# Linear attention and SwiGLU, two layers: the column sums of phi(K) from a matmul of ones, or from the gram product itself

## The chip, the cores and the metric

The kernel runs on one core of a Trainium2 chip. The core has a matrix engine (PE, TensorE), three engines for elementwise work (DVE is VectorE, ACT is ScalarE, POOL is GpSimd), a queue processor that issues the transfers (SP) and 16 DMA engines. Every engine works through its own list of instructions in order and waits on semaphores for the others. Matmuls take their operands from on-chip memory (SBUF) and write to eight banks of accumulators (PSUM).

The metric is the device time of one execution in microseconds, as the median of several runs. All times below are microseconds unless marked ns.

## What is computed

`x` has 2048 rows of 512 features. Two kinds of block are applied in turn, A, B, A, B, and each adds its result to `x`.

```python
def _A_ref(x, wqkv, wo):                       # H = 32 heads of 16
    q, k, v = ...                              # x @ wqkv, split by head
    phi = lambda t: jnp.where(t > 0, t + 1, jnp.exp(t)) + 1e-6
    pq, pk = phi(q), phi(k)
    kv = jnp.einsum("bhsd,bhse->bhde", pk, v)
    z = jnp.einsum("bhsd->bhd", pk)            # column sums of phi(K)
    num = jnp.einsum("bhqd,bhde->bhqe", pq, kv)
    den = jnp.einsum("bhqd,bhd->bhq", pq, z)[..., None] + 1e-6
    return (num / den) @ wo                    # heads put side by side again

def _B_ref(x, w1, w3, w2):
    return (silu(x @ w1) * (x @ w3)) @ w2      # 512 -> 1792 -> 512

x = x + _A_ref(layernorm(x), A_wqkv, A_wo)
x = x + _B_ref(layernorm(x), B_w1, B_w3, B_w2)
# and both once more with the same weights
```

`z`, the 512 column sums of phi(K) over the 2048 rows, is the quantity that the change is about.

## The kernel before

The rows are worked on in 16 tiles of 128. Every fp32 operand of a matmul is split into a high and a low fp16 part, and a product is three passes, high by high, low by high and high by low (`PASSES`, line 32, and `mm`, line 873). All working buffers are views of one large tile, `arena`, so most names in the profile are `arena`.

A layer of attention (`attention`, line 1244) has three stages.

*Keys.* For tile t, `keys_rows` and `keys_turn` (lines 1483 and 1491) normalise the rows (ACT, line 855), cast them to the high part (`nat[:, 0]`, POOL or ACT, lines 790 and 792), form the low part (`nat[:, 1]`, DVE or POOL, line 1497) and transpose both by DMA (line 1498). The transposed tile times the key weights is `pk` (12 matmuls of 512 columns, line 878, into the tile named `pk`). `phi_act` and `phi_sum` (lines 1222 and 1236) make phi(K) of it in three ACT instructions (lines 1228 to 1230) and one DVE instruction (line 1239). ACT scales it to its high part (line 1306), DVE makes the low part (line 1321). `gram` (line 1269) multiplies the transpose of the untransposed normalised rows `nat` by phi(K), 512 by 512 numbers added up over all 16 tiles in the four banks `gt0` to `gt3`; that is 12 matmuls of 512 columns a tile. The values never appear: since V is the normalised rows times the value weight, kv is the value weight's transpose times this gram matrix.

*The state.* The column sums, wanted in every partition, stand in the bank `pz`. `gram_sum` (line 1257) adds a tile to them on PE, as a matmul with a matrix of ones, once with the high and once with the low part. A table, `pz:` in `ENGINES` (lines 543 and 551), says for each tile who adds it: E is PE, P and V are POOL and DVE, which add phi(K) in fp32 to `pksum` (lines 1310 and 1312). In layer 0 the first 12 tiles are E and the last 4 P; in layer 1 there are 14 P and 2 V and no E. `totals` (line 1345) brings what `pksum` holds into `pz` with one fp32 matmul, which the trace shows as two instructions. From `pz` come a power of two per column that scales the gram matrix (`inverse` and `scale_gram`, lines 752 and 1359), the row `zb` for the denominators (line 1366) and the columns that scale the output weights (lines 1368, 1374, 1382). The scaled gram matrix is split (lines 1360 and 1363) and multiplied by the value weight (`kv`, 48 small matmuls of line 878), masked to heads, split again and multiplied by the output weight (`pm`).

*Queries.* Four tiles ahead, `query` makes `pq`, DVE, ACT and POOL make phi(Q), weigh it and divide it, a DMA transposes it, and `po` is the product with `pm`. Between the end of the gram and the first product with the state, PE has the first query tiles to do.

The MLP follows with 7 groups of hidden features in chunks of 512 rows, with fewer products than the plain formula has. It takes most of the time and isn't touched.

During the keys of layer 0 the weights come in from HBM and are prepared. `att_piece` (line 1979) loads the attention weights, `prepare_vo` (line 1012) finds the largest value of the value and output weights (DVE, line 720), and splits them (ACT line 800, DVE line 802). The tables `FILLS` say how many such steps follow which step of the keys; each `yield` of `prepare_vo` is one step.

The order of the instructions on every engine is written out by hand: `ORDER` (line 72) holds, for each of PE, DVE, ACT, POOL and SP, the order as a permutation of the order in which the program records them, and `arrange` (line 634) pins it. On each engine, then, a late instruction holds up all that stand behind it.

Of the kernel before, what the change touches and what calls it, by code (L numbers as in the profile page):

```python
# [8 lines left out]
F16 = mybir.dt.float16  # L9
# [441 lines left out]
def kernel(  # L451
# [792 lines left out]
    def attention(layer, ready, prep, before_gram):  # L1244
# [36 lines left out]
        for t in range(NT):  # L1281
# [8 lines left out]
            if t == lag:  # L1290
                gt.extend([acc_bank(f"gt{j}") for j in range(NK)])
                if "E" in sums:
                    pz.append(bank("pz"))
# [799 lines left out]
```

## Time and profile before

| | before |
|---|---|
| median of 3 runs | 1154.07 (1153.33 to 1154.54) |
| the profiled execution, its own time | 1151.51 |
| its span, first to last instruction | 1149.8 |
| PE busy | 1139.5 (99%) |
| DVE busy | 822.0 (71%) |
| ACT busy | 628.8 (55%) |
| POOL busy | 405.8 (35%) |
| granted TensorE clock | 1.00 |

The profiled execution took 2.56 less than the median of the runs, and 1.7 of its own time lies outside the span. Layer 0's keys run from the start to about 105, its queries to about 195, its MLP to about 590; layer 1 follows with its keys to about 669, and its last instructions are the stores of the output.

Rows of the page and of the trace name a line of the kernel, an engine, an operation, the tile written and the tiles read (`arena<-arena`), the shape and type, and the count. Rows of the timeline begin with start and duration; what ended the idle time before an instruction stands in brackets. A busy time merges overlaps: consecutive matmuls overlap in the pipeline, so a matmul's own duration (379 ns at 512 columns) is longer than the distance from one to the next.

### The profile page before, as it was taken

How to read it: one execution, taken by the hardware profiler on the slowest of the kernel's cores; microseconds unless marked ns; L12 is line 12 of the kernel's file. 1: busy time of each engine (PE TensorE's matmuls, PEld its weight loads, DVE VectorE, ACT ScalarE, POOL GpSimd, SP SyncE). 2: the span in 40 equal slices, each digit the busy share in tenths (PEclk: the TensorE clock that was granted, in tenths of full speed). 3: DMA queues.
4: the chain of work that ended last, by engine and by line, in shares of the span. 5: the costliest groups of instructions: out<-in, count | busy, mean ns of one | idle time of the engine just before them, and what ended most of it. 6: DMA issues, size and time to landing. Idle time of an engine off the chain costs nothing.

```text
span 1149.8 us, 21802 instructions
## 1 busy us (share of the span) xinstructions
PE 1139.5 (99%) x8862; PEld 864.0 (75%) x8862; DVE 822.0 (71%) x1401; ACT 628.8 (55%) x1078; POOL 405.8 (35%) x472
## 2 busy tenths in 40 slices
PE   8999999999999999999999999999999999999998
PEld 3445445888888888888854454478888888888887
DVE  6888888977878986778774467847866676556533
ACT  6587878866544554334457644776554434343422
POOL 4533688411101312212568615771153110303111
PEclk9999999999999999999999999999999999999999
DMA  9975666875854221111314715674253440022001
GB/s 277 316 231 201 183 171 129 229 170 180 242 203 182 99 84 65 65 65 66 92 32 128 216 41 122 120 172 93 77 134 116 169 174 1 28 80 101 1 19 56
DMA packets 163397, 147.43 MB, mean 128 GB/s; under 512 B 129632, under 2 KB 138976, under 8 KB 158688
## 3 DMA queue, kind: packets, MB, share of 16 engines
q1 hardware_dynamic: 163296, 146.04, 44.3%
q8 instruction: 69, 1.13, 0.4%
q14 instruction: 32, 0.26, 0.1%
HBM read 72.48 MB, written 42.07 MB: 100 GB/s over the span
## 4 chain that ended last, share of the span: by engine, by line
PE 94%; POOL 3%; DMA 1%; DVE 1%; ACT 1%; issue 0%; SPq 0%; POOLq 0%
PE bb L878 25%; PE po L1739 18%; PE bc L878 13%; PE pq L878 7%; PE po L878 7%; PE ba L878 6%; PE gt L878 6%; PE pk L878 5%; PE po L1759 4%; DMA arena<-arena 1%; DMA arena<-in_A_x_dram 1%; POOL arena L1312 0%; PE kv L878 0%; PE pm L878 0%; PE pz L1261 0%; POOL rs_all L849 0%
## 5 line engine op out<-in xcount | busy, mean ns | idle before, releaser
L878 PEld LDWEIGHTS <-arena 128*128 128x128 f16 x6360 | 617.8, 98 | 242.5 <-DMA arena<-arena 6.6
L878 PE MATMUL bb<-arena 128*128 128x256 f16 x2688 | 348.7, 273 | 0.1
L1739 PE MATMUL po<-arena 128*128 128x256 f16 x1932 | 266.7, 273 | 0.0
L1692 ACT ACTIVATE arena<-bb 128x512 f32<-128x512 f32 x196 | 115.8, 593 | 226.0 <-PE bb L878 186.5
L1739 PEld LDWEIGHTS <-arena 128*128 128x128 f16 x1932 | 189.0, 98 | 22.3
L878 PE MATMUL bc<-arena 128*128 128x256 f16 x1344 | 178.9, 273 | 0.0
L1695 DVE TENSOR_TENSOR arena<-arena,bc 128x512 f32<-128x512 f32 x112 | 76.7, 685 | 102.5 <-PE bc L878 56.6
L1653 DVE TENSOR_TENSOR arena<-arena 128x512 f16<-128x512 f32 (+1 forms) x90 | 104.4, 1162 | 32.1 <-ACT arena L1651 32.1
L1647 ACT ACTIVATE arena<-arena,scalars 128x512 f32<-128x512 f32 (+1 forms) x112 | 74.5, 666 | 96.2 <-DVE arena L1695 87.0
L1651 ACT ACTIVATE arena<-arena 128x512 f16<-128x512 f32 (+1 forms) x112 | 98.9, 886 | 33.5 <-DVE arena L1666 13.1
L1788 DVE SCALAR_TENSOR_TENSOR arena<-po,scalars,arena 128x256 f32<-128x256 f32 (+1 forms) x170 | 94.6, 584 | 27.5 <-PE po L1739 18.9
L1648 DVE SCALAR_TENSOR_TENSOR arena<-arena,scalars 128x512 f32<-128x512 f32 (+1 forms) x112 | 80.9, 723 | 39.4 <-ACT arena L1647 38.0
L878 PE MATMUL ba<-arena 128*128 128x256 f16 x672 | 92.1, 273 | 0.0
L878 PE MATMUL pk<-arena 128*128 128x512 f16 x384 | 87.8, 379 | 3.3 <-DMA arena<-arena 3.3
L878 PE MATMUL gt<-arena 128*128 128x512 f16 x384 | 88.9, 379 | 0.8 <-ACT arena L1306 0.6
L878 PE MATMUL pq<-arena 128*128 128x512 f16 x384 | 86.6, 379 | 0.0
L878 PE MATMUL po<-arena 128*128 128x512 f16 x384 | 86.5, 379 | 0.0
L1808 POOL TENSOR_TENSOR arena<-arena 128x512 f32<-128x512 f32 x25 | 34.1, 1366 | 114.7 <-DVE arena L1788 114.7
L1653 POOL TENSOR_TENSOR arena<-arena 128x512 f16<-128x512 f32 x22 | 27.0, 1225 | 124.2 <-ACT arena L1651 84.5
L1809 POOL TENSOR_TENSOR arena<-arena 128x512 f32<-128x512 f32 x25 | 37.0, 1479 | 84.0 <-DVE arena L1788 83.9
L1759 PE MATMUL po<-arena 128*128 128x256 f16 x480 | 64.8, 273 | 0.0
L855 ACT ACTIVATE arena<-arena,nb_all,rs_all 128x512 f32<-128x512 f32 x64 | 51.0, 805 | 17.4 <-POOL nb_all L852 14.4
(163 smaller groups left out, 1286.1 us busy)
## 6 DMA issues: line engine op xcount, KB each, us to landing
arena<-xb_d SPq DMA_DIRECT2D x12, 1792.0 KB, 7.7
xb_d<-arena SPq DMA_DIRECT2D x8, 1792.0 KB, 7.5
xt_d<-arena SPq DMA_DIRECT2D x32, 256.0 KB, 3.3
arena<-xt_d SPq DMA_DIRECT2D x32, 256.0 KB, 3.1
arena<-in_B_w_dram SPq DMA_DIRECT2D x8, 896.0 KB, 6.6
arena<-in_B_w_dram SPq DMA_DIRECT2D x28, 256.0 KB, 3.1
w_d<-arena SPq DMA_DIRECT2D x4, 1792.0 KB, 9.5
arena<-w_d SPq DMA_DIRECT2D x4, 1792.0 KB, 7.4
```

The lines of the kernel that those rows point to most:

```text
L855: nc.scalar.activation(dst, x_sb[:, t, :], AF.Identity, scale=rs_all[:, t : t + 1], bias=nb_all[:, t : t + 1],)
L878: nc.tensor.matmul(dst, lhs(a, k), rhs(b, k), start=first and k == 0 and i == 0, stop=last and k == n - 1 and i == len(PASSES) - 1, skip_g ...
L1647: nc.scalar.activation(t, gate, AF.Silu, scale=info["u1"])
L1648: nc.vector.scalar_tensor_tensor(t, up, info["hid"], t, OP.mult, OP.mult)
L1651: nc.scalar.activation(hs[:, 0, lo:hi], t[:, lo:hi], AF.Copy)
L1653: engine.tensor_tensor(hs[:, 1, lo:hi], t[:, lo:hi], hs[:, 0, lo:hi], OP.subtract)
L1692: nc.scalar.activation(dst, bank_, AF.Copy)
L1695: nc.vector.tensor_tensor(dst, dst, bank_, OP.add)
L1739: nc.tensor.matmul(po[:, i * HALF : (i + 1) * HALF], hs[:, a, qx, cs], w2[:, b, qw, :], start=g == ends[0] and i + a + b == 0, stop=g == e ...
L1759: nc.tensor.matmul(acc[n][:, half * HALF : (half + 1) * HALF], hs[:, a, qx, cs], w2_a21[g][:, b] if (i, half) == (0, 1) else w2[:, b, i + ...
L1788: nc.vector.scalar_tensor_tensor(dst, src, cb, to, OP.mult, OP.add)
L1809: engine.tensor_tensor(x1, x1, u[:, 1:], OP.add)
```

## The change

The gram product delivers the column sums itself. Its row for feature 0 is the sum over the rows of `nat[:, feature 0]` times phi(K). If that column of `nat` is set to ones (1 in the high part, 0 in the low part) after the tile has been transposed, row 0 of the gram matrix is the column sums of phi(K). The true row of feature 0 is then missing. It isn't needed if the value weight's first row is zero, and it can be made so: a normalised row sums to zero over its features, so subtracting one row of the weight from all its rows leaves the product as it is.

- `gram_sum`, the table `pz:` and `pksum` go, with their 24 matmuls (layer 0), 2 copies and 16 additions on POOL and 2 additions on DVE.
- `gram` begins with a copy of two numbers into each of 128 partitions of `nat`, on POOL: 16 in each layer. The first group of a tile's matmuls (`gt0`) needs it, the other three don't.
- `totals` copies the bank `gt0` to SBUF on ACT, and the fp32 matmul multiplies it by a matrix that picks its first row. Before, this matmul read `pksum`. The bank `pz` is taken there and no longer at the first tile of layer 0.
- One more DMA brings the first row of the value weight to all 128 partitions, 256 KB written, and `prepare_vo` subtracts it from the four pieces of the weight on POOL before their largest value is taken. This adds four steps to `prepare_vo`.
- Two small memsets on DVE make the pair (1, 0).
- `ORDER` is written anew for all five engines, over the whole kernel.

```diff
-            "pz:EEEEEEEEEEEEPPPP plain:YYNN ...
+            "plain:YYNN ...
...
-            "pz:PPPPPPPPPPPVVPPP plain:NNNYNNNY ...
+            "plain:NNNYNNNY ...
...
+    first_one = scalar().bitcast(F16)
+    nc.vector.memset(first_one[:, 0:1], 1.0)
+    nc.vector.memset(first_one[:, 1:2], 0.0)
...
-    pksums = view(AT_T + 2 * KB, F32, D), junk_row
...
+    v_first = view(AT_W + 8 * KB, F32, D)
...
     def prepare_vo():
         yield AT["v"]
+        for k in range(NK):
+            nc.gpsimd.tensor_tensor(st_att[2][:, k, :], st_att[2][:, k, :], v_first, OP.subtract)
+            yield 1
         yield from attn_bound("v", 2)
...
-        def gram_sum(t):
-            if sums[t] == "E":
-                pk = pks[t]
-                for a in range(2):
-                    nc.tensor.matmul(
-                        pz[0],
-                        ones16,
-                        pk[:, a, :],
...
-                    )
-
         def gram(t):
             pk, nat = pks.pop(t), nats.pop(t)
+            nc.gpsimd.tensor_copy(nat[:, :, 0], first_one)
             for j in range(NK):
...
-                if "E" in sums:
-                    pz.append(bank("pz"))
...
             def high():
                 nc.scalar.activation(pk[:, 0, :], e, AF.Copy, scale=info["tk"])
-                if sums[t] != "E":
-                    engine = engine_of("pz", t)
-                    if t == rows_of[0]:
-                        engine.tensor_copy(pksum, e)
-                    else:
-                        engine.tensor_tensor(pksum, pksum, e, OP.add)
...
         def totals():
             held["rz"] = f32()
-            if not pz:
-                pz.append(bank("pz"))
-            if rows_of:
-                factor = info["tk"].to_broadcast([P, P])
-                nc.tensor.matmul(pz[0], factor, pksum, start=len(rows_of) == NT, stop=True)
+            pz.append(bank("pz"))
+            nc.scalar.activation(junk_row, gt[0], AF.Copy)
+            pick = one_row.to_broadcast([P, P])
+            nc.tensor.matmul(pz[0], pick, junk_row, start=True, stop=True)
...
     def att_piece(i):
         src = wqkv_r[:, i] if i < 3 else wo.rearrange("(k p) n -> p k n", p=P)
+        if i == 2:
+            nc.sync.dma_start(v_first, wqkv[0:1, 2 * D :].to_broadcast([P, D]))
```

Feature 0 of a row has left the gram product by this, and only there: the keys and the queries are made from the transposed tiles, which hold all features.

More of the change, by code (lines that the diff above doesn't have):

```diff
@@ L542 @@
         (
-            "pz:EEEEEEEEEEEEPPPP plain:YYNN hid:VPVVVVPVPPVVVVPVPPPPPPPVVPVV "
+            "plain:YYNN hid:VPVVVVPVPPVVVVPVPPPPPPPVVPVV "
             "den:AVAAVVVVVAAAAAAV bq:AAVV nat:APAPAPPPPPPAAAAA key:PPPPAPPPPPPPPPAA "
@@ L550 @@
         (
-            "pz:PPPPPPPPPPPVVPPP plain:NNNYNNNY hid:VVVVVVPPVPVVVVVVVVVVPVVPPPPP "
+            "plain:NNNYNNNY hid:VVVVVVPPVPVVVVVVVVVVPVVPPPPP "
             "den:VVVVVAVVAAVVVVVV nat:AAAPPPPAPAAAAAAA key:AAAAAPPPAAAAPAAP "
@@ L1250, in attention @@
         gt, pz, pks = [], [], {}
-        sums = table_of("pz", layer)
-        rows_of = [t for t in range(NT) if sums[t] != "E"]
-        pksum = pksums[layer]
-        def gram_sum(t):
-            if sums[t] == "E":
-                pk = pks[t]
-                for a in range(2):
-                    nc.tensor.matmul(
-                        pz[0],
-                        ones16,
-                        pk[:, a, :],
-                        start=t == sums.index("E") and a == 0,
-                        stop=not rows_of and t == NT - 1 and a == 1,
-                    )
         def gram(t):
             pk, nat = pks.pop(t), nats.pop(t)
+            nc.gpsimd.tensor_copy(nat[:, :, 0], first_one)
             for j in range(NK):
@@ L1296, in attention @@
             if lag < t < LATER:
-                gram_sum(t - 1)
                 gram(t - 1)
             elif t > LATER:
-                gram_sum(t - 2)
                 gram(t - 2)
@@ L1427, in attention @@
         chain = {
-            "gram14": lambda: (gram_sum(NT - 2), gram(NT - 2)),
-            "gram15": lambda: (gram_sum(NT - 1), gram(NT - 1)),
+            "gram14": lambda: gram(NT - 2),
+            "gram15": lambda: gram(NT - 1),
             "totals": totals,
```

701 rows, old and new, of the table ORDER are left out of this document.

## The prediction

> **What bounds the kernel now.** I read the page first, then who waited for whom on PE, then the windows of layer 0's keys, and last the timeline at the places that the change touches.
>
> ```profile
> span 1149.8 us, 21802 instructions
> PE 1139.5 (99%) x8862; PEld 864.0 (75%) x8862; DVE 822.0 (71%) x1401; ACT 628.8 (55%) x1078; POOL 405.8 (35%) x472
> ...
> PE 94%; POOL 3%; DMA 1%; DVE 1%; ACT 1%; issue 0%; SPq 0%; POOLq 0%
> ```
>
> PE is busy for 99% of the span and carries 94% of the chain that ended last. In such a kernel a matmul less is worth its distance to the next one, as long as PE finds its next work ready. The waits of PE and three windows (columns: window, its length, busy time and count of PE, PEld, DVE, ACT and POOL, clock, DMA share, GB/s) say how ready it is:
>
> ```profile
> PE pk L878 <- DMA arena<-arena: 3.3, 4, 1.4
> PE gt L878 <- ACT arena L1306: 0.6, 1, 0.6
> PE gt L878 <- DVE arena L1321: 0.2, 1, 0.2
> ...
> 24.00:104.47 80.47, 80.10 (x375) 36.98 (x374) 67.98 (x130) 57.63 (x96) 31.84 (x60) 1.00 0.91 265
> 20.00:40.00 20.00, 18.18 (x84) 7.96 (x83) 12.42 (x24) 12.07 (x19) 7.10 (x19) 1.00 1.07 314
> 40.00:60.00 20.00, 20.00 (x95) 8.95 (x93) 19.07 (x34) 12.69 (x21) 8.58 (x18) 1.00 1.13 320
> ```
>
> From 24 to 104.47, which holds nearly all of layer 0's keys, PE stands still for 0.37. DVE is next: 67.98 of 80.47 busy, 12.5 idle, and 95% busy between 40 and 60. ACT has 28% idle, POOL 60%.
>
> **The change part by part.** *The matmuls of ones.* The groups of the tile `pz`, and two rows of PE's timeline that follow each other:
>
> ```profile
> L1261 PE MATMUL pz<-arena,ones x24: 378/379/379, 19.1 to 89.5; 128*128 128x512 f16 x24
> L1351 PE MATMUL pz<-arena,scalars x4: 592/592/592, 101.4 to 668.6; 128*128 128x512 f32 x4
> ...
> 89.31 0.59 PE L1261 MATMUL pz<-arena,ones 128*128 128x512 f16 x2
> 89.74 2.10 PE L878 MATMUL gt<-arena 128*128 128x512 f16 x9
> ```
>
> Two of them hold PE for 89.74 - 89.31 = 0.43, so one for 0.215, and 24 for 24 x 0.215 = 5.2. All lie between 19.1 and 89.9, where PE has next to no gaps, so all 5.2 is on the path. The fp32 pair of line 1351 stays, with another operand of the same shape: 0. Layer 1 had no matmul of ones, so PE has as many matmuls there as before.
>
> *POOL.* Its groups that go, and the nearest ones to what comes:
>
> ```profile
> L1312 POOL TENSOR_TENSOR arena<-arena 128x512 f32<-128x512 f32 x16 | 21.7, 1354 | 16.6 <-DVE arena L1239 13.1 <-DVE scalars L728 3.3
> L1310 POOL COPY arena<-arena 128x512 f32<-128x512 f32 x2 | 2.1, 1070 | 2.6 <-DVE arena L1239 2.6
> L1497 POOL TENSOR_TENSOR arena<-arena 128x512 f16<-128x512 f32 x17 | 20.2, 1188 | 9.2 <-ACT arena L790 8.8
> L848 POOL TENSOR_SCALAR ve<-mv_all 128x1 f32<-128x1 f32 x28 | 6.9, 248 | 30.4 <-DVE mv_all L841 28.6
> ```
>
> Layer 0 loses 3 additions and a copy, 3 x 1.354 + 1.07 = 5.1, and gains the 4 subtractions from the value weight, of the additions' shape, 4 x 1.354 = 5.4, and 16 copies of two numbers. No row has such a copy; 248 ns is the nearest (one number a partition), 1070 ns (512 numbers) bounds it from above, so 4.0, at most 17. POOL has 48.6 idle in the window above and takes either. Layer 1 loses 13 additions and a copy, 18.7, and gains 4.0. Both beside PE, 0 as busy time; as waits they come back below. The two additions on DVE (layer 1) and its two memsets are off the path too.
>
> *The end of the gram.* The sums now exist only when `gt0` is finished. Layer 0's end in order of time, and ACT's copy of a bank:
>
> ```profile
> 98.77 0.72 ACT L1306 ACTIVATE arena<-arena,scalars 128x512 f16<-128x512 f32 x1 [0.72 <-DVE arena L1239]
> 100.81 0.74 DVE L1321 SCALAR_TENSOR_TENSOR arena<-arena,scalars 128x512 f16<-128x512 f32 x1
> 101.41 1.02 PE L1351 MATMUL pz<-arena,scalars 128*128 128x512 f32 x2
> 102.27 3.40 PE L878 MATMUL gt<-arena 128*128 128x512 f16 x15
> 102.79 0.68 DVE L752 TENSOR_SCALAR arena<-pz 128x512 int32<-128x512 int32 x1
> 105.51 5.34 PE L878 MATMUL pq<-arena 128*128 128x512 f16 x24
> 110.69 0.95 PE L1374 MATMUL pz<-scalars,arena 128*128 128x1 f32 x8
> 112.87 1.07 DVE L1363 TENSOR_TENSOR arena<-arena 128x512 f16<-128x512 f32 x1
> 114.09 2.84 PE L878 MATMUL kv<-arena 128*128 128x128 f16 x48
> ...
> L1692 ACT ACTIVATE arena<-bb 128x512 f32<-128x512 f32 x196 | 115.8, 593 | 226.0 <-PE bb L878 186.5 <-DVE arena L1648 29.7 <-DVE arena L1666 4.3
> ```
>
> In the built program the fp32 pair stands behind tile 15's last matmul. `gt0` is that tile's first group of three, so ACT's copy (0.59) has the other nine matmuls, 9 x 0.215 = 1.9, as cover. If the cover is gone it costs up to 0.6. Four weight splits stand ahead of the copy on ACT; they delay it only if ACT itself is late; before, tile 15's high part was done at 99.49, 3.4 ahead of its first matmul at 105.51 - 12 x 0.215 = 102.9. Behind it stand the splits of the scaled gram, which need the sums anyhow. Then DVE: from the pair's start to line 752 it took 102.79 - 101.41 = 1.4, and eight instructions of 0.68 follow up to the last low part that `kv` needs: about 1.4 + 5.4 = 6.8 after the gram's end, 7.5 with ACT's first conversion. PE meanwhile has the pair (0.86), 24 matmuls of queries (5.2), the columns (0.95) and 12 more (2.6): 9.6. So `kv` finds its operands, 0; at the old spacing (113.94 - 101.41 = 12.5) it would be 2.9 late. I take 0, since the splits that stretched the old spacing stand elsewhere now.
>
> *DVE in layer 0.* Its work ahead of tile 15's low part is nearly the same, but PE wants that part sooner. Before, DVE finished it at 101.55, and PE used it at 105.51 - 10 x 0.215 = 103.4, 1.8 later. Now the pair is behind the gram and 5.2 are gone, so PE asks for it at about 97.3: DVE must come 4.2 earlier, out of 12.5 of idle time, of which a good part lies ahead of 40 (7.6 idle from 20 to 40). If it can't come earlier at all, the gram ends at 101.55 + 2.15 = 103.7 and the pair at 104.6, a gain of 0.9. Range for this term 0 to +4.3; I take 0, because the idle is three times what is asked, and in that early part the new order on DVE brings two low parts and a largest value forward.
>
> POOL and DVE can hold each other up:
>
> ```profile
> 88.89 1.65 POOL L1312 TENSOR_TENSOR arena<-arena 128x512 f32<-128x512 f32 x1 [0.91 <-DVE arena L1239]
> 89.40 1.70 DVE L802 SCALAR_TENSOR_TENSOR arena<-arena,scalars 128x512 f16<-128x512 f32 x1
> 92.50 0.74 DVE L802 SCALAR_TENSOR_TENSOR arena<-arena,scalars 128x512 f16<-128x512 f32 x1
> ```
>
> The same DVE instruction takes 1.70 beside a POOL addition that ends at 90.54 and 0.74 alone: 0.96 lost. The four subtractions could cost DVE 4 x 0.96 = 3.8, and the four POOL operations that go give as much back, so this term is 0; it belongs to the bounds above. The Trainium skill, "SBUF — State Buffer", section "Who interferes with whom", says that a DVE instruction with two SBUF inputs and a GpSimd instruction that reads SBUF exclude each other for the whole of the first. The rows agree; by that rule the 16 copies would hold DVE too, and the sum would be up to 16 x 0.25 = 4.0 worse, an estimate that supposes every copy meets such an instruction and every hold reaches PE.
>
> *Transfers.* SP gets the broadcast row, 256 KB. In the 40 to 60 window DMA is full (1.13 of 16 engines, 320 GB/s), so it takes 0.8 from whatever is behind it. On PE only the first tiles' transposes have no lead:
>
> ```profile
> 15.45 1.46 SPq L870 DMA_TRANSPOSE arena<-arena  x1
> 22.30 1.25 SPq L1498 DMA_TRANSPOSE arena<-arena  x1
> 27.55 2.76 PE L878 MATMUL pk<-arena 128*128 128x512 f16 x12 [0.37 <-DMA arena<-arena]
> ...
> 621.68 1.46 PE L878 MATMUL gt<-arena 128*128 128x512 f16 x6
> 624.16 2.76 PE L878 MATMUL pk<-arena 128*128 128x512 f16 x12 [1.02 <-DMA arena<-arena]
> 586.00:669.00 83.00, 81.98 (x393) 38.36 (x391) 40.95 (x61) 50.86 (x80) 57.23 (x78) 1.00 0.46 127
> arena<-arena SPq DMA_TRANSPOSE x96, 3.9
> ```
>
> The row is issued behind tile 4's transpose and costs those nothing. SP's new order also puts fewer tiles of x between the first transposes, but PE takes tile 2's keys before the first gram. Of the 3.3 that PE waited for transposes, 2.3 are at the start; I take 0, between -2.3 and +0.8. The last wait, 1.02, is in layer 1, where POOL is 57.23 of 83 busy and loses 18.7: -1.0 if that was why the transpose was late. Against it stands a new wait: the copy for a tile waits for its transpose, and POOL's queue stands behind it. In the new order the copy of tile 6 is directly ahead of tile 7's low part, and tile 13's of tile 14's. From tile 6's landing two copies (0.5), the low part (1.19) and the next landing (3.9) make 5.6; PE has 27 matmuls between the two tiles' keys, 5.8. So +1.0 is as possible as -1.0, and I take 0.
>
> *Sum.* -5.2 on the profiled execution: span 1149.8 to 1144.6, its own time 1151.51 to 1146.3. That execution was 2.56 faster than the median of the runs; taken off the median, 1154.07 - 5.2 = **1148.9**.
>
> **The rivals.** *A: DVE becomes the bound of layer 0's keys.* For it: 95% busy between 40 and 60, and the same work wanted 4.2 sooner. Against: 12.5 idle. If nothing of the idle can be used, 1154.07 - 0.9 = 1153.2; with half of the 4.2, 1154.07 - 5.2 + 2.1 = 1151.0. That the matmuls of ones stood in gaps and their removal does nothing (1154.07) is the far end of this; the 0.37 of gaps speaks against it.
>
> *B: POOL's copies close a loop, and it ends slower.* Landing, copy, next low part, next landing: in layer 1, from tile 6 to 14, each tile would take L + 1.7 for a landing L, in place of 24 x 0.215 = 5.2. At the 5.2 that the transpose issued at 22.30 took (PE's keys behind it start at 27.55) the loss is 9 x 1.7 = 15.3, and the time 1154.07 - 5.2 + 15.3 = 1164.2. It decides from L = 4.3 up (9 x 0.83 = 7.5, 2.3 slower than before). The median landing of 3.9 and the order, which ties only two neighbours so, speak against it; with these two, 2 x 1.7, it is 1152.3.
>
> *C: the waits go as well.* All 3.3 of waits for transposes vanish: 1154.07 - 5.2 - 3.3 = 1145.6.
>
> **How the numbers follow.** The forecast (a gain of 4 to 7) 0.60, A 0.17, B 0.10, C 0.10, other 0.03. A measurement of this kernel tells about 0.2% from no change, 2.3. A falls half on a gain above that, half within; B is slower in seven of ten, the rest within. Faster 0.60 + 0.10 + 0.08 + 0.02 for the rest = 0.80, same 0.12, slower 0.08. The range runs from C's 1145.6 to 1152.6, which takes in the forecast, C, and A's nearer part.
>
> **What would show it.** Right: PE with 24 matmuls less and 1134.3 busy, layer 0's queries beginning on PE at about 100, no wait of PE for line 1321's low part, and none at the fp32 pair. Wrong: waits of `gt` for DVE or POOL between 30 and 100 (A), waits of `pk` for transposes in layer 1 with POOL's two-number copies waiting for DMA (B), or a wait of `kv` behind the new sums. What the forecast rests on most is that the new order elsewhere keeps PE as full as the old one.

## The result and the profile after

The changed kernel takes 1150.89 (median of 22 runs, 1149.66 to 1153.24). The kernel before, in runs taken beside these, takes 1152.38 (22 runs, 1151.34 to 1154.54). The ratio is 0.9988, with a 95% interval from 0.9983 to 0.9994: 1.5 faster, real but below the 0.2% that was taken as the bound. The forecast was 1148.9 with a gain of 5.2. So the direction and the range hold, and seven tenths of the gain are missing. The three runs that the forecast was taken off had a median of 1154.07, 1.7 above that of the 22; so the forecast time misses by only 2.0, and it is the gain that has to be explained.

The page of the changed kernel, first the span and the busy times, then the shares of the chain that ended last:

```profile
span 1149.1 us, 21795 instructions
PE 1135.3 (99%) x8838; PEld 860.9 (75%) x8838; DVE 811.8 (71%) x1401; ACT 633.6 (55%) x1080; POOL 391.3 (34%) x490
...
PE 87%; DVE 4%; POOL 3%; DMA 2%; ACT 2%; issue 1%; SPq 0%; POOLq 0%; DVEq 0%; ACTq 0%
```

PE has its 24 matmuls less, and its share of the chain has gone from 94% to 87%: at more places than before another engine or a DMA released it. Its waits still come to only some 10 in all. Its waits in the changed kernel by what ended them (in total, times, longest):

```profile
PE pk L886 <- DMA arena<-arena: 4.8, 4, 2.1
PE bb L886 <- DMA arena<-arena: 1.2, 1, 1.2
...
PE pk L886 <- DVE arena L776: 0.8, 1, 0.8
PE bc L886 <- DVE arena L1680: 0.6, 1, 0.6
PE po L886 <- DMA arena<-arena: 0.2, 1, 0.2
```

The wait of `pk` for transposes was 3.3 in four places, 2.2 of it in the first 50 and 1.0 in layer 1. Now it is 4.8, all in the first 50, and the one in layer 1 is gone. New are 1.2 and 0.6 in layer 0's MLP (lines 886 and 1680, at 224.20 and 205.50). The 0.8 of `pk` for DVE, at 16.01, stands in place of 0.8 that `gt` waited for ACT and DVE before. Where PE's time went shows in one window of either kernel, from 24 to 50. Before:

```profile
24.00:50.00 26.00, 25.63 (x119) 11.44 (x118) 19.21 (x32) 17.01 (x27) 12.14 (x28) 1.00 1.12 310
```

and after:

```profile
24.00:50.00 26.00, 22.25 (x102) 9.84 (x103) 15.61 (x27) 15.12 (x25) 14.46 (x31) 1.00 1.07 322
```

PE is busy 3.38 less in the same 26. The DMA engines are full in both (1.12 and 1.07 of 16 engines, 310 and 322 GB/s). PE's timeline of the changed kernel in that stretch and at the end of the gram:

```profile
24.64 5.35 PE L886 MATMUL pk<-arena 128*128 128x512 f16 x24 [0.94 <-DMA arena<-arena]
29.83 5.34 PE L886 MATMUL gt<-arena 128*128 128x512 f16 x24
37.25 2.76 PE L886 MATMUL pk<-arena 128*128 128x512 f16 x12 [2.07 <-DMA arena<-arena]
39.85 0.81 PE L886 MATMUL gt<-arena 128*128 128x512 f16 x3
41.69 2.76 PE L886 MATMUL pk<-arena 128*128 128x512 f16 x12 [1.03 <-DMA arena<-arena]
...
102.42 1.02 PE L1336 MATMUL pz<-arena,scalars 128*128 128x512 f32 x2
103.28 5.34 PE L886 MATMUL pq<-arena 128*128 128x512 f16 x24
...
111.85 2.84 PE L886 MATMUL kv<-arena 128*128 128x128 f16 x48
```

The queries of layer 0 begin at 103.28 instead of 105.51, and `kv` at 111.85 instead of 114.09: 2.2 is what is left of the 5.2 at this place. SP's timeline of the changed kernel says what the transposes at 37.25 and 41.69 stood behind:

```profile
24.10 0.42 SPq L1962 DMA_DIRECT2D arena<-in_A_x_dram  x1
24.58 0.44 SPq L1967 DMA_DIRECT2D arena<-in_A_wqkv_dram  x1
25.06 0.44 SPq L1500 DMA_DIRECT2D xt_d<-arena  x1
25.55 1.44 SPq L1962 DMA_DIRECT2D arena<-in_A_x_dram  x3
27.03 0.76 SPq L1969 DMA_DIRECT2D arena<-in_A_wo_dram  x1
27.83 0.68 SPq L901 DMA_DIRECT2D arena<-in_B_w_dram  x1
28.62 3.61 SPq L1483 DMA_TRANSPOSE arena<-arena  x1
```

The transpose of tile 5 is issued at 28.62, directly behind four tiles of x, the broadcast row (line 1967), a store, a piece of the output weight and an 896 KB block, and its keys begin at 37.25, 8.6 later; the median landing before was 3.9.

### The profile page after: what moved, and what is told of

Read it like the earlier page. It is cut to its first block, busy times and chain, and to the rows that moved or that the text cites. A ratio compares the mean times of both kernels' runs of the same rounds, so it can differ in the third digit from the quotient of the medians.

```text
span 1149.1 us, 21795 instructions
## 1 busy us (share of the span) xinstructions
PE 1135.3 (99%) x8838; PEld 860.9 (75%) x8838; DVE 811.8 (71%) x1401; ACT 633.6 (55%) x1080; POOL 391.3 (34%) x490
## 3 DMA queue, kind: packets, MB, share of 16 engines
q8 instruction: 69, 1.13, 0.4%
## 4 chain that ended last, share of the span: by engine, by line
PE 87%; DVE 4%; POOL 3%; DMA 2%; ACT 2%; issue 1%; SPq 0%; POOLq 0%; DVEq 0%; ACTq 0%
PE bb L886 24%; PE po L1724 18%; PE bc L886 12%; PE gt L886 6%; PE ba L886 6%; PE pk L886 6%; PE pq L886 5%; PE po L1744 4%; PE po L886 4%; DMA arena<-arena 2%; DVE arena L810 1%; POOL arena L1563 1%; PE kv L886 0%; PE pm L886 0%; ACT arena L808 0%
## 5 line engine op out<-in xcount | busy, mean ns | idle before, releaser
L1632 ACT ACTIVATE arena<-arena,scalars 128x512 f32<-128x512 f32 x112 | 74.6, 666 | 89.5 <-DVE arena L1680 84.4
L1633 DVE SCALAR_TENSOR_TENSOR arena<-arena,scalars 128x512 f32<-128x512 f32 x112 | 80.8, 721 | 39.8 <-ACT arena L1632 39.3
L1648 POOL TENSOR_TENSOR arena<-arena 128x256 f32<-128x256 f32 x10 | 7.6, 765 | 145.4 <-DVE arena L1633 145.4
```

The source lines that it names most:

```text
L1632: nc.scalar.activation(t, gate, AF.Silu, scale=info["u1"])
L1633: nc.vector.scalar_tensor_tensor(t, up, info["hid"], t, OP.mult, OP.mult)
```

## The experiments

The theory formed on this is F: until about 85 the transfers are the bound just behind PE, since everything that layer 0's keys load passes through DMA engines that are full. A transpose then lands when the bytes ahead of it are through, and PE's work that is taken away ahead of such a landing turns into waiting. Its rivals: the removal is worth its full price and the new order elsewhere lost it (R); something else just behind PE paces the keys, ACT and DVE with phi and the low part (G). Each run is told with its median beside that of the kernel before on the same chip (1152.42, 1152.22 and 1152.21 for the runs of the three groups that were taken together). `kv` is the start of that stage in layer 0, one profiled execution each.

**The 24 matmuls of ones alone, in the old order.** In `gram_sum` the two matmuls are left out (`leave_out` notes them, and the positions in `ORDER` are closed up):

```diff
         def gram_sum(t):
             if sums[t] == "E":
                 pk = pks[t]
+                if True:
+                    leave_out("PE", 2)
+                    return
                 for a in range(2):
...
-                nc.tensor.matmul(pz[0], factor, pksum, start=len(rows_of) == NT, stop=True)
+                nc.tensor.matmul(pz[0], factor, pksum, start=True, stop=True)
```

> The kernel before with its old order on all engines, without the 24 matmuls of ones in layer 0 (the first 12 tiles are left out of layer 0's column sums). It does the removal alone. Theory S (the start is paced by the landings of the transposes, and a matmul that is gone ahead of such a landing turns into waiting): PE's waits for transposes before 50 grow from 2.2 to between 3 and 4, the fp32 pair begins 3 to 4.3 earlier than before (97.1 to 98.4), and the whole is 3 to 4.3 faster than before, which is more than the 2.2 that the changed kernel has at that place: the rest of its loss is then the new order's. Rival R (the removal is worth its full price in the old order, and all that is missing is the new order's): 4.7 to 5.2 faster, the waits as before. Rival N (the removal is worth only what the changed kernel shows): 1 to 2.3 faster.

Measured: 1151.25 (12 runs), ratio 0.9992 [0.9983, 1.0002], 1.2 less than the kernel before. PE's timeline of this run follows. The kernel before has no wait on PE between 28 and 100:

```profile
34.04 2.76 PE L891 MATMUL pk<-arena 128*128 128x512 f16 x12 [0.89 <-DMA arena<-arena]
38.09 2.76 PE L891 MATMUL pk<-arena 128*128 128x512 f16 x12 [0.64 <-DMA arena<-arena]
43.22 2.76 PE L891 MATMUL pk<-arena 128*128 128x512 f16 x12 [0.42 <-DMA arena<-arena]
58.11 2.76 PE L891 MATMUL pk<-arena 128*128 128x512 f16 x12 [0.47 <-DMA arena<-arena]
...
113.26 2.84 PE L891 MATMUL kv<-arena 128*128 128x128 f16 x48
```

Four transposes that were just in time are now late. In the kernel before they had landed 1.0, 0.4, 0.2 and 0.05 ahead of PE's first matmul on them (issue and time to landing by line 1498). `kv` is 0.83 earlier for 5.2 of work less. (In this execution the clock was also at 0.67 from 10 to 12 and 0.50 from 12 to 14, and the first keys began at 13.10 instead of 11.93; by the keys of tile 2 a shorter wait had made this good, 21.97 against 21.82, so it doesn't explain the 0.83.) R falls: the old order alone loses most of the gain. Rival N's time is met, but its ground isn't: what is lost is lost without any of the new order. Three of the late transposes are issued within 0.2 of the old times (28.63, 32.13 and 37.14), though PE is ahead, and take 5.4 to 6.0 from issue to landing instead of 4.4 to 5.3, which speaks for F. But SP itself waited for DVE's low part of the rows ahead of the first (1.7), so the making of the rows has a part in it that no run shows apart.

**The same 24 put back into the changed kernel.** They are recorded behind the first group of a tile and placed behind it on PE:

```diff
+            for a in range(2 if layer == 0 and t < 12 else 0):
+                ADDED.append(made_by("PE"))
+                nc.tensor.matmul(gt[0], ones16, pk[:, a, :], start=False, stop=False)
```

> The changed kernel with 24 matmuls of ones put back into layer 0, two behind each of the first 12 tiles' first group, written onto the bank gt0, so that its gram matrix is no longer right. Theory S: those ahead of the late transposes at 37.25 and 41.69 fall into PE's waits and cost nothing (about 6 to 8 of the 24), the rest cost 0.215 each: 3.4 to 3.9 slower than the changed kernel, with PE's waits for transposes down from 4.8 to about 3.3. Rival R: 5.2 slower, the waits unchanged. If the waits had nothing to do with PE's own pace: also 5.2.

Measured: 1154.75 (11 runs), ratio to before 1.0023 [1.0014, 1.0032]; 3.9 above the changed kernel, `kv` at 115.58 (3.73 later). The waits for transposes fall from 4.8 to 3.0:

```profile
PE pk L900 <- DMA arena<-arena: 3.0, 4, 1.4
```

This is theory S's forecast (3.4 to 3.9). In the new order, then, the removal is worth 3.8 to 3.9 of its 5.2; and the rest of the change, with the 24 in place, makes the kernel 2.3 slower than before.

**Fewer bytes, with and without the 24.** In the kernel before, the stores of the first 8 transposed tiles of layer 0 are left out:

```diff
             i, ap = kept.pop(0)
+            if i < 8 and i not in unstored:
+                unstored.append(i)
+                leave_out("SP")
+                continue
             nc.sync.dma_start(xt_d[:, i], ap)
...
-        nc.sync.dma_start(xqs[t], xt_d[:, t])
+        other = t + 8 if t < 8 and t not in read else t
+        read.append(t)
+        nc.sync.dma_start(xqs[t], xt_d[:, other])
```

> The kernel before without the stores of the first 8 transposed tiles (8 x 256 KB) in layer 0; the queries of these tiles read the tiles 8 to 15 in their place, so the output is not the reference's. It takes 2.1 MB out of the first 75, and nothing comes back later. Theory F: the waits for transposes at the start (2.2) fall to 0.5 to 1.5, kv begins 0.7 to 1.8 earlier than in the kernel before (112.3 to 113.4). It is there for the comparison with the next.

Measured: 1151.10 (11 runs), ratio 0.9988 [0.9979, 0.9997]. The waits ahead of 24 did not fall (1.5 at 22.17), since few stores stand ahead of them, and `kv` came only 0.2 earlier; both parts of the expectation missed. But from 24 to 105 PE has no gap at all:

```profile
24.00:105.00 81.00, 81.00 (x380) 37.61 (x379) 68.75 (x132) 57.65 (x96) 31.88 (x60) 1.00 0.87 243
```

> The kernel of the run before this one without the 24 matmuls of ones (the first 12 tiles are left out of layer 0's column sums as well). Theory F (the removal is eaten where transposes are late because of the bytes that stand ahead of them): with 2.1 MB less it is worth 2.5 to 4.5, against 0.8 at kv and 1.2 in the whole with all bytes. Rival G (something else just behind PE, ACT and DVE with phi and the low part, paces layer 0's keys): 0.8 to 1.5 as before.

Measured: 1148.63 (5 runs), ratio 0.9964 [0.9951, 0.9976], 2.5 below the run without the stores alone. The keys of tile 2 and `kv` of the first and of the second:

```profile
22.17 2.76 PE L891 MATMUL pk<-arena 128*128 128x512 f16 x12 [1.52 <-DMA arena<-arena]
...
113.88 2.84 PE L891 MATMUL kv<-arena 128*128 128x128 f16 x48
```
```profile
21.09 2.76 PE L891 MATMUL pk<-arena 128*128 128x512 f16 x12 [1.36 <-DMA arena<-arena]
...
110.79 2.84 PE L891 MATMUL kv<-arena 128*128 128x128 f16 x48
```

The same removal is worth 0.83 at `kv` with all bytes and 3.09 with 2.1 MB less. But 1.08 of the 3.09 is there at the keys of tile 2 (21.09 against 22.17), where only two of the 24 can have counted (0.43). From those keys on it is 2.0, against 1.0 with all bytes. By the medians it is 2.5 (95% interval 1.6 to 4.5) against 1.2 (-0.5 to 2.1). This speaks for F, whose range began at 2.5, and against G, but the two intervals overlap, so the difference isn't clear of noise. PE still waits for a transpose at 41.38 (1.11) and for a low part of DVE at 86.88 (0.70); the second is G's wait, in the second place.

**The bytes moved instead of taken.** Six of the eight 896 KB blocks of the MLP's weights go behind 59 on SP (the new `ORDER["SP"]` isn't shown); all largest values are taken from the first block:

```diff
-                abs_max(bounds[n][:, i : i + 1], st_w13[:, b // 4, c, k, half])
+                abs_max(bounds[n][:, i : i + 1], st_w13[:, 0, 0, 0, half])
```

> The kernel before with six of the eight 896 KB blocks of the MLP's weights moved on SP from the first 58 to between 59 and 85; the largest values are taken from the first block six more times in place of theirs, so that the scales are not the right ones; DVE has as many instructions as before. It takes 4.5 MB out of the stretch in which the DMA engines are full. Theory F: PE's waits for transposes at the start (2.2) go, kv begins 1.5 to 2 earlier (112.1 to 112.6), unless the late blocks make a wait after 100. It is there for the comparison with the next.

Measured: 1158.43 (5 runs), 6.2 above before. The start is free from 24 on (PE busy for 26.00 of the 26 up to 50), but what was moved comes back. From 75 to 105:

```profile
75.00:105.00 30.00, 25.88 (x114) 11.40 (x113) 23.12 (x48) 21.65 (x37) 10.12 (x13) 0.94 0.95 316
```

The DMA engines are now full there (0.95, 316 GB/s). PE waits 7.0 for transposes in the whole run, 4.7 of it from 74 to 99. The expected `kv` of 112.1 to 112.6 was missed by far (120.05). The clock of 0.94 comes back below.

> The kernel of the run before this one without the 24 matmuls of ones (the first 12 tiles are left out of layer 0's column sums as well). Theory F (the removal was eaten in the old order by transposes that land late because the DMA engines are full): with the light start it is worth nearly its price, kv 4 to 5 earlier than in the run before this one, and the whole 3.5 to 5 faster than it. Rival G (the keys of layer 0 are paced by ACT and DVE just behind PE, whatever the transposes do): 0.8 to 2 faster, with gt waiting for ACT or DVE. In the full start it was worth 0.8 at kv and 1.2 in the whole.

Measured: 1158.97 (5 runs), 0.5 above the run with the 24: worth nothing. Both expectations missed, and the trace says why. Two of PE's keys, of tiles 13 and 15, in the first run (with the 24), and the same in the second:

```profile
82.21 4.45 PE L878 MATMUL pk<-arena 128*128 128x512 f16 x12 [2.17 <-DMA arena<-arena]
...
98.72 2.76 PE L878 MATMUL pk<-arena 128*128 128x512 f16 x12 [1.23 <-DMA arena<-arena]
```
```profile
80.88 4.06 PE L891 MATMUL pk<-arena 128*128 128x512 f16 x12 [3.38 <-DMA arena<-arena]
...
98.45 2.76 PE L891 MATMUL pk<-arena 128*128 128x512 f16 x12 [3.06 <-DMA arena<-arena]
```

Without the 24, PE comes to the last of these 3.06 - 1.23 + 0.27 = 2.1 sooner and waits that much longer: the transpose lands at the same time within 0.27. It lands 3.0 and 3.1 behind its issue in the two runs; what is late is the issue (95.64 and 95.31), for which SP waits 6.3 and 7.9 on the landing of a store issued directly behind two of the moved blocks. Here work that is taken away turns into waiting in full, as F says, though not at the place where it was looked for.

**The broadcast row.** The changed kernel without the row and the four subtractions:

```diff
-            nc.gpsimd.tensor_tensor(st_att[2][:, k, :], st_att[2][:, k, :], v_first, OP.subtract)
+            leave_out("Pool")
...
-            nc.sync.dma_start(v_first, wqkv[0:1, 2 * D :].to_broadcast([P, D]))
+            leave_out("SP")
```

> The changed kernel without the broadcast row (256 KB) and without the four subtractions on POOL: the value weight keeps its first row, so the output is not the reference's. Theory F: the row is 0.8 us of full DMA engines ahead of the two late transposes (it is issued at 24.58, they at 28.62 and 34.18), so that its absence is worth 0.5 to 0.9; the subtractions are worth nothing. Rival: the row and the subtractions cost nothing, as the prediction said: 0.

Measured: 1149.31 (11 runs), ratio to before 0.9974 [0.9966, 0.9983]; against before 2.9 faster, where the changed kernel is 1.5: 1.4 for the two (1.6 by the medians as they stand, 95% interval 1.3 to 2.4). SP's and then PE's timeline of this run:

```profile
27.73 3.26 SPq L1496 DMA_TRANSPOSE arena<-arena  x1
...
33.05 2.42 SPq L1496 DMA_TRANSPOSE arena<-arena  x1
```
```profile
36.28 2.76 PE L899 MATMUL pk<-arena 128*128 128x512 f16 x12 [1.05 <-DMA arena<-arena]
38.89 0.81 PE L899 MATMUL gt<-arena 128*128 128x512 f16 x3
39.53 2.75 PE L899 MATMUL pk<-arena 128*128 128x512 f16 x12
```

The two late transposes are issued 0.9 and 1.1 sooner, the keys of tile 5 begin 1.0 and those of tile 6 2.2 sooner. The first subtraction of the changed kernel runs at 45.65, behind both; so up to here it is the row's doing. `kv` is 1.42 earlier (110.43). It is more than the 0.8 of its bytes that the expectation gave. The subtractions were not tried alone.

Two ways to have the row without its 256 KB, with nothing left out. First a broadcast on POOL:

```diff
+        added("Pool")
+        nc.gpsimd.partition_broadcast(v_first, st_att[2][0:1, 0, :])
         for k in range(NK):
             nc.gpsimd.tensor_tensor(st_att[2][:, k, :], st_att[2][:, k, :], v_first, OP.subtract)
...
-        if i == 2:
-            nc.sync.dma_start(v_first, wqkv[0:1, 2 * D :].to_broadcast([P, D]))
```

> The changed kernel with the value weight's first row brought to all partitions by a broadcast instruction on POOL, from the partition where the row already stands, in place of the 256 KB transfer; the subtractions stay, nothing is left out. Theory F (it was the 256 KB in a stretch of full DMA engines that made the run without row and subtractions 1.6 faster than the changed kernel): 1.2 to 1.8 faster than the changed kernel, 1149.1 to 1149.7. Rival H (the four subtractions on POOL were the price): as the changed kernel, 1150.9. If the broadcast or what it needs holds POOL for several us, the high and low parts behind it are late and the time is longer.

Measured: 1163.44 (4 runs), 11.2 above before. POOL's timeline of this run, and the instructions of POOL's sequencer (POOLq) at these two lines:

```profile
52.01 0.80 POOL L1036 PARTITION_BROADCAST arena<-arena  x1 [7.77 <-DMA arena<-in_A_wqkv_dram]
59.88 1.25 POOL L1038 TENSOR_TENSOR arena<-arena 128x512 f32<-128x512 f32 x1 [7.07 <-issue]
...
L1036 POOLq MODIFY_POOL_CONFIG  x2: 11/11/11, 44.2 to 44.2; - x2
L1038 POOLq MODIFY_POOL_CONFIG  x2: 129/129/129, 52.7 to 52.8; - x2
```

The broadcast itself takes 0.80, but POOL stands still for 7.77 ahead of it and for 7.07 behind it, and PE waits 12.8 for a low part. Both stretches begin at a MODIFY_POOL_CONFIG, at 44.2 ahead of the broadcast and at 52.7 behind it; no other run has one. The profile puts the first down to the load that brings the row, but in the changed kernel the first subtraction reads the same load at 45.65. So a change of POOL's configuration, there and back, is the likely price; no run shows it apart. The run says nothing on the row's price.

Then four rows of 2 KB and a shuffle on DVE:

```diff
+    added("DVE")
+    nc.vector.memset(v_first, 0.0)
...
+        added("DVE")
+        nc.vector.stream_shuffle(v_first, v_first, [0] * 32)
...
-            nc.sync.dma_start(v_first, wqkv[0:1, 2 * D :].to_broadcast([P, D]))
+            for p in range(0, P, 32):
+                nc.sync.dma_start(v_first[p : p + 1], wqkv[0:1, 2 * D :])
```

> The same with four transfers of one row each (2 KB, to partitions 0, 32, 64 and 96) and a shuffle on DVE that copies each within its 32 partitions, with one memset more on DVE; nothing is left out. It stands behind the low part at 38.35, where DVE is idle. Theory F: 1.0 to 1.8 faster than the changed kernel, 1149.1 to 1149.9; three more issues on SP (3 x 0.45) ahead of the late transposes may take some of it. Rival H: as the changed kernel.

Measured: 1151.93 (11 runs), ratio to before 0.9996 [0.9987, 1.0005], about 1 above the changed kernel. Both theories missed. SP's timeline of this run, then PE's:

```profile
26.00 1.29 SPq L1985 DMA_DIRECT2D arena<-in_A_wqkv_dram  x4
27.33 2.28 SPq L1979 DMA_DIRECT2D arena<-in_A_x_dram  x3
30.28 0.33 SPq L1987 DMA_DIRECT2D arena<-in_A_wo_dram  x1
30.65 0.43 SPq L916 DMA_DIRECT2D arena<-in_B_w_dram  x1
31.19 1.61 SPq L1500 DMA_TRANSPOSE arena<-arena  x1
```
```profile
40.13 4.45 PE L901 MATMUL pk<-arena 128*128 128x512 f16 x12 [4.01 <-DMA arena<-arena]
```

There are 248 KB less and three issues more, and tile 5's transpose is issued at 31.19 instead of 28.62. About 0.8 of these 2.6 lie ahead of the edit: in this execution (1153.35, slower than the median) DVE waits 1.0 at 8.44 for a piece of the key weight, and tile 4's transpose is issued at 21.36 instead of 20.59. The other 1.8 is SP's queue. The four issues take 1.29 where one took 0.44, and SP issues no transfer before the eighth ahead of it has landed: the load at 30.28 begins 0.02 behind the landing of the store issued at 25.55, the eighth ahead of it, and in the changed kernel's trace none of the 327 transfers goes against this. So three issues more push the loads behind them against such landings. Bytes, then, are not the whole of F: SP's queue has a part in it, and how the row's 1.4 divides between the two isn't shown.

**Another order of the transfers.** Only `ORDER["SP"]` of the changed kernel is edited. The first:

```diff
-        "0-7 12 21 11 8-9 25 19 18 20 22-23 10 27 24 26 37 28 30 17 42 45 29 31-32 36 48 34 40 13 "
-        "39 59 38 82 54 43-44 35 14 33 41 16 52 49 55 50 47 58 53 15 51 57 60 46 56 67 61-62 81 "
+        "0-7 12 21 11 8-9 22 19 18 20 23 10 27 25 24 26 37 28 30 17 31-32 42 29 34 13 36 45 38 43 "
+        "54 40 48 39 44 35 59 82 14 33 41 16 52 49 55 50 47 58 53 15 51 57 60 46 56 67 61-62 81 "
```

> The changed kernel with another order of SP's transfers up to the 45th, nothing else: the transposes of tiles 3 to 7 go ahead of loads that are used late in the trace (a 896 KB block used at 51.8, two 256 KB pieces of the output weight used at 64.6 and 69.7, tiles of x used at 47 to 50; of two blocks, the one used at 23.8 goes first, the one used at 35.1 behind tile 4's transpose). Theory S: the waits of PE for transposes before 50 fall from 4.8 to between 1 and 2, the fp32 pair begins about 3 earlier (99.4), and the whole is 2.5 to 3.5 faster than the changed kernel. Rival F (the DMA engines are full and only the sum of bytes counts, so that the wait moves to another transfer): same as the changed kernel, within 0.7, with the wait elsewhere in the first 80.

Measured: 1152.27 (11 runs), ratio to before 0.9997 [0.9989, 1.0006]: no better than the changed kernel, and by the medians 1.4 slower. The waits at 37 and 41 are gone, as was wanted, and a new one stands at 55 (the timeline, then a window behind it):

```profile
55.41 4.24 PE L886 MATMUL pk<-arena 128*128 128x512 f16 x12 [2.01 <-DMA arena<-arena]
```
```profile
57.00:60.00 3.00, 3.00 (x9) 1.07 (x8) 2.12 (x3) 0.31 (x1) 2.84 (x6) 0.51 1.08 334
```

So rival F of that run was right in that the wait moved; its time, within 0.7, was missed. In this execution the wait that moved brings more with it: the clock is at half (0.51) for the next 3, and 12 matmuls take 4.24 instead of 2.76. But this was the fastest of the eleven (1151.05), and seven of the others were at a full clock and slower, so the clock doesn't explain the 1.4, and what does isn't shown.

One more swap, in layer 0's MLP:

```diff
-        "120 118 121-126 129 128 131 138 137 132 130 143 142 133-134 127 139 154 153 151 135 150 "
+        "120 118 121-126 129 128 131 138 137 132 130 133 143 142 134 127 139 154 153 151 135 150 "
```

> The kernel of the run before this one, with one more swap on SP: in layer 0's MLP the transpose that stood behind two loads of weights, which wait for DVE at 214.9, goes ahead of them. Theory: the wait of PE for a transpose at 224.2 (1.16) goes, 1.0 to 1.3 faster than the kernel without this swap. Rival: the two loads are late in its place, ACT and then PE wait for them, and the time is the same or longer by up to 1.

Measured: 1151.56 (11 runs), 0.7 below the run before it, which is within what these runs can tell. The wait for the transpose at 224 (0.6 in the run before this one) is gone, and ACT's wait for the two loads has come in its place, as the rival said:

```profile
225.93 0.50 PE L1744 MATMUL po<-arena 128*128 128x256 f16 x3 [1.15 <-ACT arena L1636]
```

Last, the loads by the time at which they are read:

```diff
-        "0-7 12 21 11 8-9 25 19 18 20 22-23 10 27 24 26 37 28 30 17 42 45 29 31-32 36 48 34 40 13 "
...
+        "0-7 12 21 11 8-9 22 19 18 10 20 23 26-27 25 24 28 30-31 17 32 34 13 37-38 43 36 29 42 54 "
...
```

> The changed kernel with the transfers from the 14th to the 70th in another order on SP: each load by the time at which the trace of the changed kernel first reads what it brings (9 us ahead of it, 12 for the 896 KB blocks), the transposes by the time at which their rows are ready. So about 1.8 MB (parts of the query, value and output weights and a tile of x, read at 58 to 76) go behind 55. Theory F (to about 60 the DMA engines are full; the moving of some 1 MB only shifted the wait from 37 to 55, and what helps is to take bytes out of the first 55): PE's waits for transposes in the first 60 fall from 4.8 to between 0.5 and 2, kv begins 2 to 4 earlier (108 to 110 against 111.85), 1148 to 1149.5. Rival G (the keys have a second bound just behind the transposes, the way from ACT over DVE to the low part): the waits for transposes fall, but gt waits for DVE or ACT in their place, and the time is within 0.7 of the changed kernel's.

Measured: 1156.05 (5 runs), 3.8 above before. PE is busy for all of 24 to 50, and then waits 4.36 at 77.13 for a transpose that stands behind what was pushed back:

```profile
77.13 5.22 PE L886 MATMUL pk<-arena 128*128 128x512 f16 x12 [4.36 <-DMA arena<-arena]
```

None of the three orders beats the changed kernel. What is put off in the first 50 is wanted before 85 and stands in the way of a later transpose.

## Why the prediction was right in direction and wrong in size

Against the kernel before on the same chips the change is 1.5 faster. With the 24 put back it is 2.3 slower, so the removal is worth 3.8 in the new order; the row and the subtractions take 1.4 back, and 0.9 is left for the rest: -3.8 + 1.4 + 0.9 = -1.5. The parts are not independent of each other and each is uncertain by several tenths, so this is a reading of three measurements, not a law.

- *The matmuls of ones, "so all 5.2 is on the path".* This is the term that failed first. Its size on PE was nearly right: 24 x 0.215 = 5.2, and PE is busy for 4.2 less. The ground was wrong: PE stood still for only 0.37 from 24 to 104, and from this it was concluded that PE sets the pace. A hand-made order that brings each transpose just in time shows the same picture. Without the 24 the transposes are late, and by the medians the removal is worth 1.2 in the old order (0.83 at `kv`), 2.5 with 2.1 MB less, 3.8 in the new order, and nothing where the DMA engines are full up to 105. The quoted rows had the sign: the DMA share of 1.13 from 40 to 60, and the 3.3 that PE's keys waited for transposes. The landings would have shown it: ahead of tile 9's keys (57.99) stood 14 of the 24, 3.0 of work, and the transpose of that tile had landed 0.05 ahead of its use.
- *The broadcast row, "costs those nothing".* It is behind tile 4's transpose, as said (24.58 against 20.59), but it is ahead of those of tiles 5 and 6, which have no lead either. Taken as 0.8 "from whatever is behind it" and then as 0; with the subtractions it measured 1.4.
- *The transposes at the start, taken as 0 between -2.3 and +0.8.* The waits in the first 50 went from 2.2 to 4.8, +2.6, outside these ends. The upper end came from the row alone; that the new order puts 2.9 MB between the transposes of tiles 4 and 5 (four tiles of x, the row, two stores, a piece of the output weight and a block) was not costed.
- *The wait in layer 1, taken as 0 between -1.0 and +1.0.* It is gone, -1.0. It stays, at 1.0 and more, in every run built on the kernel before that still has POOL's additions there, and is in none built on the changed one. POOL's relief and the new order were not tried apart.
- *Layer 0's MLP.* It was not in the prediction. Two new waits, 1.16 at 224.20 and 0.58 at 205.50, and 0.2 in the queries; less the 1.0 of layer 1 this is 0.9, as much as the rest above. That it is the same 0.9 isn't shown: with the 24 put back, where the rest was measured, these waits are 0.9, none and 0.3, and the swap that took the first away gained nothing clear of noise.
- *POOL's work: 0.* The sizes were right (copies 293 ns where 248 was taken, subtractions 1292 where 1354 was). PE waits for no copy in this trace (once, 0.70 at 62.66, in the run with the loads by the time they are read). The copies do wait for transposes (8.3 in five places), and transposes on SP for copies (7.6 in three), as rival B said, but its loop doesn't reach PE: no wait of `pk` in layer 1. The rule that was weighed there, from the Trainium skill, "SBUF — State Buffer", section "Who interferes with whom", would have made the sum up to 4.0 worse by 16 copies holding DVE up. This trace doesn't show it: PE's only wait for DVE in layer 0's keys, 0.83 at 16.01, is ahead of the first copy (18.32). No run took the copies away.
- *The end of the gram: 0.* Right. No wait at the fp32 pair (102.42) and none at `kv`, which begins 9.4 after the pair where 9.6 of PE's work was counted.
- *DVE in layer 0: 0, rival A.* Right as far as the changed kernel goes: `gt` waits for DVE nowhere from 30 to 100. Without the 24 in the old order it does once, 0.7 at 89; so A's bound lies close behind the transposes.
- *What would show it.* PE's queries at "about 100" came at 103.28, its 1134.3 came out as 1135.3. The last sentence of the prediction, that the new order keeps PE as full as the old one, is the one that decided, and it was left without a price.

## What to carry to other kernels

An engine that is busy for 99% of a stretch isn't shown to be its bound: look how long before each use its operands land, and count a removed instruction only as far as the next operand is there sooner. Where the DMA engines are full, price an added transfer by the transposes or loads behind it in the queue, by its bytes and by its issue. Changing the order of the transfers moved such a wait here; what made it smaller was taking transfers out (the row, or the stores).

## What the runs showed of the hardware that was not expected

A wait of PE of about 2 us can cost 1.5 or more again behind it, and need not. The 2.01 ahead of 55.41 in the first order of transfers was followed by a granted clock of 0.51 from 57 to 60, and 12 matmuls took 4.24 instead of 2.76; behind the 4.01, 4.36 and 2.17 quoted above they took 4.45, 5.22 and 4.45. But the 2.07 ahead of 37.25 in the changed kernel left the clock at 1.00, and so did the 3.06 ahead of 98.45 in the light start without the 24 (2.76 for its 12 matmuls). The Trainium skill, "TensorE: Matmul & The Clock Gate", section "What's actually happening", says that the clock falls to half after an idle window of about 3.4 us and comes back after as much sustained work. The length of the slow stretch agrees in the first order of transfers (0.85 from 55.4 to 57, 0.51 to 60, 1.00 behind it, about 3.4 at half); that an idle time of 2.0 was enough here is shorter than the window it gives.

A broadcast instruction of POOL among its ordinary ones, with a MODIFY_POOL_CONFIG ahead of it and one behind it, made POOL stand still for 7.77 ahead of it and 7.07 behind it, against 0.80 for itself.

The issue of a transpose on SP, 1.2 to 1.3 when the queue is light, takes 3.61 at 28.62 of the changed kernel, behind the block and the loads; SP's queue itself is then late for all that follows.
